# A decode block on one core: the last V loaded behind its predecessor, quads in fours, and gate and up computed as rows

## The chip, the cores and the metric

One core of one Trainium2 chip runs the whole program. The time is the device time of one execution in microseconds. A profiled execution also has a "span", from the first instruction to the last, which is about 2 us shorter than the time (659.4 for 661.2). All moments below, such as "650.3", are us from the start of the span.

## The reference, cut to what matters

It is one decode step for two sequences: layer norm, attention over a cache, output projection, layer norm, gated MLP.

```python
B, Sq, D = 2, 1, 512
Hq, Hkv, Sk, Dh = 32, 32, 8192, 128      # k_cache, v_cache: (2, 32, 8192, 128) bf16
F = 1376
q = layernorm(x) @ wq                    # wq (512, 4096)
p = softmax(q k^T * Dh ** -0.5)
h = x + (p v) @ wo                       # wo (4096, 512)
gate = layernorm(h) @ W_gate             # (512, 1376)
up = layernorm(h) @ W_up
out = h + (relu(gate) * up) @ W_down     # W_down (1376, 512)
```

There is one query per head, so the work is to read the cache once. The program reads 281.06 MB.

## The kernel before

The heads are handled in 16 "quads" (four heads of one sequence). Each quad has a K tile and a V tile of 8.4 MB each, 64 KB on every partition. VectorE (DVE) multiplies K by the query and folds the product down; ScalarE (ACT) takes the exponentials; TensorE (PE) multiplies them with V. There are two buffers for K and one for V.

```python
for n in range(N - 1):                        # N = 16
    scores(n, HALVES if n == 0 else (0, T))   # DVE: product, 4 folds, a reduction; ACT: exponentials
    if n + 2 < N:
        load_k(n + 2)
    collect()                                 # DVE + PE: eviction of a finished pair of quads
    # ... (row sums and gathers at certain n)
    weighted_v(n)                             # PE: 64 matmuls of 512 columns
    if n + 2 < N:
        load_v(n + 1)
# K buffer of quad 14, now free: wo, then the last V in four pieces, then gate, up, W_down
# ... (loads of wo: three blocks and one with 1 KB rows)
CUTS = (0, T // 2, T * 7 // 8, T * 15 // 16, T)
load_v(N - 1, CUTS)
# ... (loads of W_gate, W_up, W_down)
scores(N - 1)
# ... 28 of 32 "wo rows", then the pieces of the last V; its last eighth with V as the weights:
v_stationary(N - 1, o_b, CUTS[3], T)
normalize_last(L, o_b, zil)
for h in range(G):
    project(wol[:, h, :], ol[:, h, :], last=(h == G - 1))
```

A "wo row" is one matmul of the output projection: 512 columns of wo move past the attention output of the two tokens (tile `ar_ps`). The sum is then turned into columns (`a_ps` before, `h_ps` in the changed kernel), and layer norm and gate follow. `W` and `X` are the buffers of the weights that are loaded late. The last quad of each sequence is a special case: its own row sums, its own projection, and columns instead of rows. The MLP computes gate and up as columns: each 128x128 block of the weights is loaded as PE's stationary operand, and the two tokens are its moving columns. So the activations come out as W_down's product needs them.

```python
def mlp_in(g, ps):                            # 44 matmuls with two moving columns
    for c in range(KC):
        for fc in range(FC):
            # ...
            nc.tensor.matmul(out=ps[0:w, fc, :], lhsT=lhsT, rhs=hd[:, c, :], ...)
mlp_in(0, gate_ps); var = variance(hd_f, "ln2"); mlp_in(1, up_ps)
# ... relu, product
for fc in range(FC):                          # "y rows": 11 blocks of W_down, 4 matmuls each
    y_rows(act[0:w, fc, :], (wd_sb[:, fc, :] if fc < NF else wd_l[0:w]), last=(fc == FC - 1))
```

The softmax here doesn't subtract the row's maximum and nothing guards it: scores larger than these inputs give would overflow.

## Time and profile before

| before | value |
|---|---|
| time, median of 3 runs (661.32 to 661.61) | 661.44 us |
| span of the profiled run | 659.4 us |
| main DMA queue busy | 98.9% of the span |
| DVE busy | 92% |
| PE busy | 18% |

These are lines of the page: the span, the engines, the DMA queue, and the costliest group of DVE with its time, mean, and the idle time just before it.

```profile
span 659.4 us, 3234 instructions
...
PE 119.5 (18%) x1341; PEld 58.6 (9%) x1341; DVE 609.6 (92%) x225; ACT 55.8 (8%) x142; POOL 2.5 (0%) x8
...
q1 hardware_dynamic: 7272, 281.06, 98.9%
...
L222 DVE TENSOR_TENSOR k<-k,qrep 128x32768 bf16<-128x32768 bf16 (+1 forms) x17 | 275.7, 16217 | 8.9 <-DMA k<-in_A_k_cache_dram 8.8
```

Two resources look nearly full. The last line decides between them: DVE waited 8.8 us in all for K. The transfers are the bound.

The windows view of the same kernel shows the rate (the last number) in the loop and near the end; the number before it is the DMA share, and before that PE's granted clock, as a share of full speed.

```profile
core 0: us, PE busy (x) PEld busy (x) DVE busy (x) ACT busy (x) POOL busy (x), PEclk, DMA share, GB/s
40.00:554.00 514.00, 79.09 (x854) 35.70 (x854) 503.10 (x133) 38.46 (x104) 0.00 (x0) 0.57 1.00 433
645.00:650.00 5.00, 4.01 (x86) 3.10 (x79) 1.99 (x8) 0.00 (x0) 0.00 (x0) 0.78 0.97 399
650.00:655.00 5.00, 4.41 (x111) 4.10 (x114) 1.37 (x10) 0.00 (x0) 0.00 (x0) 0.50 0.71 269
```

433 GB/s is the steady rate of the loop, and close to the most there is: the Trainium skill, "DMA: Bandwidth & Descriptors", section "Specifications", gives 435 GB/s as the ceiling of the fabric, and the measured 433 agrees. 281.06 MB at 433 GB/s is 649 us. Only some 10 us of the span are left, for the start and for the end.

These are lines of the timeline before (start, duration, engine, line, operation, what ended the wait).

```profile
595.47 17.23 DVE L222 TENSOR_TENSOR k<-k,qrep 128x32768 bf16<-128x32768 bf16 x1 [1.24 <-DMA k<-in_A_k_cache_dram]
...
650.34 1.71 PE L510 MATMUL gate_ps<-hd,W 128*128 128x2 bf16 x44 [0.25 <-DVE hd L493]
652.34 1.72 PE L510 MATMUL up_ps<-hd,W 128*128 128x2 bf16 x44
654.09 0.24 DVE L528 TENSOR_TENSOR act<-gate,up_ps 96x2 bf16<-96x2 f32 x2 [0.94 <-PE up_ps L510]
654.38 1.55 PE L466 MATMUL y_ps<-W,act 128*2 128x128 bf16 x40 [0.33 <-DVE act L528]
655.76 0.28 PE L466 MATMUL y_ps<-wd_l,act 96*2 96x128 bf16 x4
656.09 0.29 DVE L535 CAST y_row<-y_ps 128x128 bf16<-128x128 f32 x1 [1.76 <-PE y_ps L466]
```

Two things end together. The chain of computation reaches the y rows at 654.38. The last full rows of W_down were issued at 641.99 and landed 13.5 us later, at 655.5; by the trace's landing records (the moments at which each of the 16 DMA engines reports its part of a load) the final 96 rows came at 655.7.

### The profile page before, as it was taken

The page shows a single profiled execution, that of the slowest core. Times are in us where ns is not written, and L with a number is a line of the kernel's source. Part 1 is how long each engine was busy: PE and PEld are TensorE (multiplying, and loading weights), DVE is VectorE, ACT ScalarE, POOL GpSimd, SP SyncE. Part 2 cuts the span into 40 slices and gives each one's busy share as a digit, 9 for nine tenths or more (in the row PEclk, how much of TensorE's full clock was granted, in tenths as well). Part 3 has the DMA queues.
Part 4 walks back from the last instruction along what each step waited for, and adds up shares of the span by engine and source line. Part 5 has one row for each costly group of instructions (what it writes and reads, how often), then busy time and mean ns, then how long its engine had stood idle before and what let it go on. Part 6 is the DMA issues. An engine that isn't in the chain of part 4 may idle for free.

```text
span 659.4 us, 3234 instructions
## 1 busy us (share of the span) xinstructions
PE 119.5 (18%) x1341; PEld 58.6 (9%) x1341; DVE 609.6 (92%) x225; ACT 55.8 (8%) x142; POOL 2.5 (0%) x8
## 2 busy tenths in 40 slices
PE   2100302003030210303012130301202030020446
PEld 1000101001010100101001110100001010010225
DVE  2899999999999999999999999999999998999952
ACT  2201001010101001010101001010010101001020
POOL 1000000000000000000000000000000000000000
PEclk9555755757565575756557575555757555575656
DMA  9999999999999999999999999999999999999996
GB/s 382 445 445 445 395 433 446 437 445 418 417 445 437 441 442 398 445 445 426 441 417 433 445 422 441 437 417 441 426 441 441 421 438 426 433 441 433 393 420 259
DMA packets 7314, 281.26 MB, mean 427 GB/s; under 512 B 802, under 2 KB 1412, under 8 KB 2308
## 3 DMA queue, kind: packets, MB, share of 16 engines
q1 hardware_dynamic: 7272, 281.06, 98.9%
q8 instruction: 10, 0.16, 0.1%
q14 instruction: 4, 0.03, 0.0%
q10 hardware_dynamic: 28, 0.01, 0.0%
HBM read 281.06 MB, written 0.00 MB: 426 GB/s over the span
## 4 chain that ended last, share of the span: by engine, by line
DVE 62%; DMA 33%; PE 3%; issue 1%; ACT 0%; DVEq 0%
DMA k<-in_A_k_cache_dram 31%; DVE k L222 29%; DVE k L228 28%; DVE sc L231 4%; DMA wq_sb<-in_A_wq_dram 2%; DVE osb L268 1%; DVE qrep L188 1%; PE qps L175 1%; PE o L257 1%; PE ar_ps L452 0%; ACT qrep L186 0%; PE y_ps L466 0%; PE a_ps L459 0%; PE gate_ps L510 0%; PE up_ps L510 0%
## 5 line engine op out<-in xcount | busy, mean ns | idle before, releaser
L222 DVE TENSOR_TENSOR k<-k,qrep 128x32768 bf16<-128x32768 bf16 (+1 forms) x17 | 275.7, 16217 | 8.9 <-DMA k<-in_A_k_cache_dram 8.8
L228 DVE TENSOR_TENSOR k<-k 128x16384 bf16<-128x16384 bf16 (+3 forms) x68 | 266.8, 3923 | 2.3
L257 PE MATMUL o<-v,pm 128*32 128x512 bf16 x1016 | 88.1, 522 | 395.8 <-DMA v<-in_A_v_cache_dram 395.8
L234 ACT ACTIVATE pm<-sc 32x256 bf16<-32x256 f32 x64 | 47.2, 738 | 563.9 <-DVE sc L231 527.6
L257 PEld LDWEIGHTS <-pm 128*32 128x32 bf16 x1016 | 37.9, 127 | 444.8 <-issue 282.3
L231 DVE TENSOR_REDUCE sc<-k 128x256 f32<-128x2048 bf16 (+1 forms) x17 | 36.7, 2161 | 1.6
L307 PE MATMUL rep<-osb,spread 128*64 128x128 f32 (+1 forms) x16 | 5.9, 474 | 110.5 <-DVE osb L268 110.5
L234 ACT ACTIVATION_READ_ACCUMULATOR pm<-sc 32x1 f32 x64 | 15.0, 234 | 0.0
L307 PEld LDWEIGHTS rep<-osb,spread 128*64 128x64 f32 (+1 forms) x16 | 3.2, 257 | 114.1 <-DVE osb L268 114.1
L188 DVE CAST qrep<-qps 32x512 bf16<-32x512 f32 x8 | 5.5, 692 | 7.2 <-ACT qrep L186 7.1
L266 DVE TENSOR_SCALAR osb<-o,turn_of 128x128 f32<-128x128 f32 x10 | 3.4, 344 | 9.2 <-PE o L257 9.2
L268 DVE SCALAR_TENSOR_TENSOR osb<-o,turn_of,osb 128x128 f32<-128x128 f32 x30 | 10.5, 351 | 1.1
L175 PE MATMUL qps<-wq_sb,xnb 128*64 128x512 bf16 x32 | 6.5, 562 | 7.0 <-DMA wq_sb<-in_A_wq_dram 4.8
L186 ACT ACTIVATE qrep<-qps 32x512 bf16<-32x512 f32 x8 | 4.7, 586 | 8.5 <-PE qps L175 5.2
L152 DVE COPY xc<-x_ps 128x8 f32<-128x8 f32 x1 | 0.2, 167 | 4.9 <-PE x_ps L149 4.9
L510 PEld LDWEIGHTS <-W 128*128 128x128 bf16 (+1 forms) x88 | 3.8, 126 | 0.3 <-issue 0.3
L175 PEld LDWEIGHTS <-xnb 128*64 128x64 bf16 x32 | 2.7, 147 | 10.0 <-issue 5.3
L452 PE MATMUL ar_ps<-W,oc 128*2 128x512 bf16 x28 | 3.2, 626 | 1.8 <-DVE oc L357 1.8
L297 PE MATMUL o_l<-lane_of,osb 128*128 128x4 f32 x2 | 0.6, 364 | 12.8 <-DVE osb L268 12.8
L317 DVE TENSOR_TENSOR rep<-rep,pick 128x128 f32<-128x128 f32 x6 | 1.8, 295 | 1.0 <-PE rep L307 0.9
L330 PE MATMUL zb<-zm,same 128*128 128x4 f32 (+2 forms) x12 | 2.3, 306 | 0.3 <-DVE ol_f L298 0.3
L330 PEld LDWEIGHTS zb<-zm,same 128*128 128x128 f32 x12 | 2.1, 258 | 0.8 <-issue 0.4
(92 smaller groups left out, 44.3 us busy)
## 6 DMA issues: line engine op xcount, KB each, us to landing
k<-in_A_k_cache_dram SPq DMA_DIRECT2D x2, 4096.0 KB
wq_sb<-in_A_wq_dram SPq DMA_DIRECT2D x1, 4096.0 KB, 12.3
v<-in_A_v_cache_dram SPq DMA_DIRECT2D x1, 4096.0 KB, 13.3
v<-in_A_v_cache_dram SPq DMA_DIRECT2D x1, 3072.0 KB, 20.2
W<-in_A_wo_dram SPq DMA_DIRECT2D x1, 2048.0 KB
W<-in_B_W_gate_dram SPq DMA_DIRECT2D x1, 1376.0 KB
W<-in_B_W_up_dram SPq DMA_DIRECT2D x1, 1032.0 KB, 27.4
W<-in_A_wo_dram SPq DMA_DIRECT2D x1, 1024.0 KB, 29.0
```

What stands on the lines that cost most here:

```text
L175: nc.tensor.matmul(out=qps[h * B * Q:(h + 1) * B * Q], lhsT=xnb[:, c].rearrange("p b q -> p (b q)"), rhs=wq_v[:, c, g:g + QP, h0 + h, :], ...
L186: nc.scalar.activation(out=dst, in_=src, func=ACT.Copy)
L188: nc.vector.tensor_copy(dst, src)
L222: nc.vector.tensor_tensor(out=kp, in0=kp, in1=_view(qrep[:, b, i, :], 0, [[0, hi - lo], [1, Dh]]), op=ALU.mult)
L228: nc.vector.tensor_tensor(out=kp[:, :, 0:half], in0=kp[:, :, 0:half], in1=kp[:, :, half:width], op=ALU.add)
L231: nc.vector.tensor_reduce(out=sc[:, lo:hi], in_=kp[:, :, 0:8], axis=AXIS.X, op=ALU.add)
L234: nc.scalar.activation(out=p_of[ps, :, :, h], in_=sc[ps, :].rearrange("p (g t) -> p g t", t=TG), func=ACT.Exp, accum_out=(zm[ps, b, i:i + ...
L257: nc.tensor.matmul(out=o[g:g + W2], lhsT=_view(pm, (0 if lane else R) + t // TG * W2, [[1, W2]]), rhs=vt[:, t:t + TG, :].rearrange("p t d ...
L268: nc.vector.scalar_tensor_tensor(out=osb, in0=o[:, t * Dh:(t + 1) * Dh], scalar=turn_of[:, t:t + 1], in1=osb, op0=ALU.mult, op1=ALU.add)
L307: nc.tensor.matmul(out=reps[where][at:at + m, max(k - 1, 0), :], lhsT=spread[n_of].rearrange("k u h m -> k (u h m)"), rhs=osb, start=True, ...
L330: nc.tensor.matmul(out=zb, lhsT=lhsT, rhs=z, start=True, stop=True)
L510: nc.tensor.matmul(out=ps[0:w, fc, :], lhsT=lhsT, rhs=hd[:, c, :], start=(c == 0 and fc == 0), stop=(c == KC - 1), skip_group_check=True)
```

## The change

Its intent is a simpler tail. The special last quad goes away: all quads are evicted in pairs and gathered in fours. To keep the last V off the end, each half of it is loaded as soon as PE has used the same half of its predecessor; wo then comes last before the MLP weights. The last K is scored in 3/4 and 1/4. Gate and up are computed as rows (the tokens stationary, 512 weight columns moving, three column groups side by side) and transposed by seven small matmuls.

```diff
-        weighted_v(n)
         if n + 2 < N:
-            load_v(n + 1)
+            weighted_v(n)
+            load_v(n + 1, (0, T) if n + 3 < N else HALVES)
@@ the last V, then wo (was: wo, then the last V)
+    vts[L] = vts[L - 1]
+    CUTS = (0, T // 2, T * 7 // 8, T)
+    for lo, hi in zip(HALVES[:-1], HALVES[1:]):
+        weighted_v(L - 1, lo, hi)
+        for a, b in zip(CUTS[:-1], CUTS[1:]):
+            if lo <= a < hi:
+                load_part(vts[L], A_v_cache, L, a, b)
+    for k in range(NGR):
+        load_wo(k)
@@ eviction of a pair
-        nc.vector.tensor_scalar_mul(osb, o[:, 0:Dh], turn_of[:, 0:1])
-        for t in range(1, TG):
-            nc.vector.scalar_tensor_tensor(...)
+        nc.vector.tensor_tensor(out=om..., in0=o..., in1=_view(turn_of, 0, [[1, TG], [0, Dh]]), op=ALU.mult)
+        nc.vector.tensor_reduce(out=osb, in_=om.rearrange("p (t d) -> p d t", d=Dh), ...)
@@ the MLP weights: a buffer of their own, the last K's, free only after its scores
+    X = kring.tile([P, RING], bf16, tag="k", name="X")
@@ MLP
+    def mlp_in(g, ps, c0=0, c1=KC):
+        for c in range(c0, c1):
+            for j in range(FT):
+                nc.tensor.matmul(out=ps[j * Q:(j + 1) * Q, :], lhsT=hd[:, c]...,
+                                 rhs=wgu[:, g, c, offs[j]:offs[j] + MT], ...)
+    ... seven matmuls act_ps <- act, ident; act_t = copy of act_ps on ACT
# cut: masks, row sums, the removed special cases of the last quad
```

## The prediction

> **What bounds the kernel now.** The DMA queue, for nearly the whole span. The page's queue table has the main queue busy for 98.9% of the span; the windows view gives 433 GB/s and DMA share 1.00 from 40 to 554 us, with a K or V load always outstanding. 281.06 MB at 433 GB/s is 649 us. DVE is 92% busy, but its first product of the last K (timeline, 595.47 us) waited for its DMA: one K takes DVE about 36 us, one K plus V takes DMA about 38.7. So only the end, or a hole in the queue, can change the time.
>
> **The tail before.** The last K lands at 595.4, V14 at 614.9, V15's last piece near 644.5, gate at 648.7, up at 652, the last W_down block near 655.5 (issue plus time to landing). From 636.4 PE is the chain: 28 wo rows 3.16, V15's first pieces, a_ps 2.0, the last V and projection until 649.1, mean, gate 1.71, variance, up 1.71 (ends 654.06), act, y rows 1.7, cast (ends 656.4), output to 659.4. Chain and DMA end within a microsecond of each other, so moving loads cannot gain more than about 1 us.
>
> **What the change does.**
> - Head: fewer mask and copy instructions on DVE, about 1.5 us. Worth 0: K2's issue still finds V0 in flight for 8 us.
> - Loop: the four evictions per pair (0.34+1.12 us) become a product and a reduce. DVE is not the bound: worth 0.
> - V15 follows V14 half by half; wo comes after it. V15's first half is issued near 609, before V14's second half lands at 615. V15 lands near 634.5, wo near 644.3; fewer short rows (the 1 KB wo rows go) may give 0.5 us. Gate, up and W_down now need the last K's buffer, free near 632, while the queue is full until 644: no hole.
> - The last K in 3/4 and 1/4: exponentials end near 634.5, V15's matmuls near 636.5, before wo's second half. Slack.
> - After wo: 16 rows 1.8, copy 0.7, h_ps 2.0, mean 0.8, hd 0.3: gate starts near 650.3, as before (650.34).
> - Gate and up as rows: each 12 matmuls of 512 columns, three side by side; at the measured 0.43 us per round of four, 4 x 0.43 = 1.7 each. As before.
> - Added: the product is 96x512 instead of 128x22, 0.6 for 0.24; seven transposes, 0.25+0.7+0.2; an ACT copy 0.3. About 1.8 us, all on the chain, because the y rows wait for it. W_down's last block has then landed.
>
> **Sum.** Before 659.4 span; +1.8 for row form and transposes; −0.5 for DMA; −0.5 because part of gate or up may run at the fast clock. The Trainium skill, "TensorE: Matmul & The Clock Gate", Part 1, puts warming at about 3.4 us of sustained work; this trace shows rounds of 0.43 us from 636.4 turning to 0.22 near 641. Predicted time 662.3 us, range 660.3 to 664.3; faster by over 2% 0.01, within 2% 0.98, slower 0.01.
>
> **What would show it.** Queue share about 0.99 and loop K issues 38.7 us apart as before; last V15 landing near 634.5; wo near 644; gate start near 650; first y row near 656 instead of 654.4; cast end near 658.
>
> **What would make it wrong.** A hole in the queue around 608 to 634 (V15 waiting for V14's halves) would add its length. If PE is fast from 645 on, gate and up halve and the kernel gains about 1 us instead.

## The result, and the profile after

The changed kernel takes 661.89 us (median of 6 runs, 661.39 to 662.11), the kernel before 661.38 in the same rounds. The ratio is 1.0006, with a 95% interval of 0.9993 to 1.0019. Here and below a ratio is the mean time of one kernel's runs over the mean of the other's in the same rounds, so it is not quite the ratio of the medians that are quoted.

The page after, the same lines as before, and one more (q8) that the last section needs:

```profile
span 660.1 us, 2931 instructions
...
PE 121.1 (18%) x1210; PEld 52.4 (8%) x1210; DVE 604.0 (92%) x163; ACT 59.6 (9%) x157; POOL 3.3 (1%) x14
...
q1 hardware_dynamic: 6600, 281.06, 98.8%
q8 instruction: 9, 0.15, 0.1%
...
L215 DVE TENSOR_TENSOR k<-k,qrep 128x32768 bf16<-128x32768 bf16 (+3 forms) x18 | 275.9, 15327 | 11.9 <-DMA k<-in_A_k_cache_dram 11.9
```

DVE does 5.6 us less and waits 3.1 us longer for K: what the loop gained went into a wait. The bytes are the same, and so is their rate, in the windows view after:

```profile
40.00:554.00 514.00, 78.23 (x844) 33.25 (x844) 500.96 (x102) 38.59 (x104) 0.00 (x0) 0.57 1.00 433
645.00:650.00 5.00, 4.04 (x30) 2.76 (x22) 0.44 (x3) 0.78 (x2) 0.00 (x0) 0.50 0.99 403
650.00:655.00 5.00, 4.21 (x31) 1.31 (x28) 2.55 (x8) 0.00 (x0) 0.00 (x0) 0.50 0.65 247
```

PE's clock, 0.78 from 645 to 650 before, is now 0.50. The end, in the timeline after:

```profile
644.17 1.88 PE L411 MATMUL ar_ps<-W,oc 128*2 128x512 bf16 x16 [3.14 <-DMA W<-in_A_wo_dram]
...
650.07 1.89 PE L456 MATMUL gate_ps<-X,hd 128*32 128x512 bf16 x12
...
652.30 1.89 PE L456 MATMUL up_ps<-X,hd 128*32 128x512 bf16 x12
...
654.24 0.68 DVE L474 TENSOR_TENSOR act<-gate,up_ps 96x512 bf16<-96x512 f32 x1 [0.70 <-PE up_ps L456]
...
655.69 1.34 PE L446 MATMUL y_ps<-X,act_t 128*2 128x128 bf16 x44 [0.28 <-ACT act_t L491]
657.08 0.29 DVE L497 CAST y_row<-y_ps 128x128 bf16<-128x128 f32 x1 [2.16 <-PE y_ps L446]
```

| moment | before | after | after minus before |
|---|---|---|---|
| last piece of the last V landed (landing records) | 644.5 | 634.2 | −10.3 |
| second half of wo landed (PE goes on) | long before | 644.1 | |
| first gate matmul | 650.34 | 650.07 | −0.27 |
| product of gate and up starts | 654.09 | 654.24 | +0.15 |
| first y row | 654.38 | 655.69 | +1.31 |
| last rows of W_down landed (landing records) | 655.7 | 655.7 | 0 |
| cast starts | 656.09 | 657.08 | +0.99 |
| end of span | 659.4 | 660.1 | +0.7 |

The last V is there 10 us earlier, and gate starts only 0.27 us earlier. wo took the last V's place as the thing that PE waits for. From gate to the first y row the row form takes 5.62 us instead of 4.04. Before, the rows ran into W_down's landing and finished 1.71 us after they began; after, they began when W_down had just come, and took 1.39.

### The profile page after: what moved, and what is told of

Read it like the earlier page. It is cut to its first block, busy times and chain, and to the rows that moved or that the text cites. A ratio compares the mean times of both kernels' runs of the same rounds, so it can differ in the third digit from the quotient of the medians.

```text
span 660.1 us, 2931 instructions
## 1 busy us (share of the span) xinstructions
PE 121.1 (18%) x1210; PEld 52.4 (8%) x1210; DVE 604.0 (92%) x163; ACT 59.6 (9%) x157; POOL 3.3 (1%) x14
## 3 DMA queue, kind: packets, MB, share of 16 engines
q1 hardware_dynamic: 6600, 281.06, 98.8%
## 4 chain that ended last, share of the span: by engine, by line
DMA 83%; PE 15%; ACT 0%; issue 0%; DVE 0%; SPq 0%
DMA v<-in_A_v_cache_dram 77%; PE o L249 13%; DMA W<-in_A_wo_dram 4%; DMA wq_sb<-in_A_wq_dram 2%; PE qps L166 1%; PE h_ps L423 0%; PE y_ps L446 0%; PE ar_ps L411 0%; PE up_ps L456 0%; ACT qrep L177 0%; PE gate_ps L456 0%; DVE qrep L179 0%; DVE act L474 0%; SPq L190 0%; ACT ar L419 0%
## 5 line engine op out<-in xcount | busy, mean ns | idle before, releaser
L215 DVE TENSOR_TENSOR k<-k,qrep 128x32768 bf16<-128x32768 bf16 (+3 forms) x18 | 275.9, 15327 | 11.9 <-DMA k<-in_A_k_cache_dram 11.9
L221 DVE TENSOR_TENSOR k<-k 128x4096 bf16<-128x4096 bf16 (+6 forms) x72 | 267.4, 3714 | 2.5
L249 PE MATMUL o<-v,pm 128*32 128x512 bf16 x1024 | 94.0, 544 | 415.9 <-DMA v<-in_A_v_cache_dram 408.2
L208 ACT ACTIVATE pm<-sc 32x256 bf16<-32x256 f32 (+2 forms) x68 | 48.1, 708 | 562.7 <-DVE sc L226 561.3
L226 DVE TENSOR_REDUCE sc<-k 128x256 f32<-128x2048 bf16 (+2 forms) x17 | 36.7, 2161 | 1.6
L292 PE MATMUL rep<-osb,spread 128*64 128x128 f32 x16 | 5.1, 421 | 101.5 <-DVE osb L262 101.5
L179 DVE CAST qrep<-qps 32x512 bf16<-32x512 f32 x4 | 2.8, 696 | 10.7 <-ACT qrep L177 10.7
L262 DVE TENSOR_REDUCE osb<-om 128x128 f32<-128x512 f32 x8 | 8.2, 1026 | 0.3
L258 DVE TENSOR_TENSOR om<-o,turn_of 128x512 f32<-128x512 f32 x8 | 5.5, 684 | 3.2 <-PE o L249 3.2
L177 ACT ACTIVATE qrep<-qps 32x512 bf16<-32x512 f32 x12 | 7.0, 588 | 5.1 <-PE qps L166 4.9
```

What stands on the lines that cost most here:

```text
L177: nc.scalar.activation(out=dst, in_=src, func=ACT.Copy)
L208: nc.scalar.activation(out=p_of[ps, lo // TG:hi // TG, :, h], in_=sc[ps, lo:hi].rearrange("p (g t) -> p g t", t=TG), func=ACT.Exp, accum_o ...
L215: nc.vector.tensor_tensor(out=kp, in0=kp, in1=_view(qrep[:, b, i, :], 0, [[0, hi - lo], [1, Dh]]), op=ALU.mult)
L221: nc.vector.tensor_tensor(out=kp[:, :, 0:half], in0=kp[:, :, 0:half], in1=kp[:, :, half:width], op=ALU.add)
L226: nc.vector.tensor_reduce(out=sc[:, lo:hi], in_=kts[n][:, lo:hi, 0:8], axis=AXIS.X, op=ALU.add)
L249: nc.tensor.matmul(out=o[g:g + W2], lhsT=_view(pm, (0 if lane else R) + t // TG * W2, [[1, W2]]), rhs=vt[:, t:t + TG, :].rearrange("p t d ...
```

## The experiments

The theory that was tested is called "two ends meet". The y rows need the chain of computation and the landing of W_down, and both come at about 655.5, so neither the row form nor a shorter chain can move the time by its full length. The main rival says that one of the two sets the end alone. Other runs test the order of the loads, the slack of DVE, and PE's clock. Each run was timed beside the kernel before on the same chip; that one took 661.33 in the first and third job and 661.28 in the second.

### Gate and up as columns in the changed kernel

```diff
-                nc.tensor.matmul(out=ps[j*Q:(j+1)*Q, :], lhsT=hd..., rhs=wgu[:, g, c, offs[j]:offs[j]+MT])
+                nc.tensor.matmul(out=ps[0:w, fc, :], lhsT=<128x128 block of wgu>, rhs=hd[:, c, :])
-    # seven transposes, copy on ACT
```

> The changed kernel with gate and up in the old column form (44 matmuls with two moving columns each, no transposes). Theory (two ends meet: the y rows need both the compute chain and the landing of W_down at 655.5 to 655.7 us): first y row near 654.2, but the last rows wait for the landing, cast ends near 656.2, time about 0.6 to 0.9 us below the changed kernel, near 661.1. Rival (the chain alone sets the end, W_down has long landed): the full 1.5 us come off, near 660.4.

Measured: 660.96 us (660.81 to 661.05), ratio to before 0.9994 (0.9982 to 1.0007). Its timeline:

```profile
654.13 1.74 PE L439 MATMUL y_ps<-X,act_t 128*2 128x128 bf16 x44 [0.33 <-DVE act_t L474]
655.92 0.29 DVE L481 CAST y_row<-y_ps 128x128 bf16<-128x128 f32 x1 [1.84 <-PE y_ps L439]
```

The first y row comes 1.56 us earlier than in the changed kernel, but the cast only 1.16. The rows take 1.74 instead of 1.34, because the last ones meet W_down, which landed at 655.5. The time is 0.93 below the changed kernel's median, though that one was timed in another job. The theory gave 0.6 to 0.9, the rival 1.5. This is the fastest correct version. All its five runs lie below all nine of the kernel before, but by 0.4 us, and the interval includes 1. It is no win that one could claim.

### Gate and up as rows in the kernel before

The reverse edit: row form and transposes, with before's loads and attention. (The query tile, gate, and three small tiles share buffers to fit.)

> The kernel before with only gate and up as rows and the seven transposes; loads and attention as before. Theory: gate starts near 650.5, first y row near 656 (1.6 us later than before), all of W_down has landed by then, time about 1 us above before, near 662.4. Rival (the transposes hide behind W_down's landing): same time as before, 661.4.

Measured: 661.64 us median, ratio 1.0013 (1.0001 to 1.0026). The five runs fall in two groups, 661.3 to 661.6 (three runs) and 663.1 to 663.4 (two), and the profile is of the second. None is within half a microsecond of the theory's 662.4, and the first group is near the rival's 661.4. These are the first half of the last V, gate and the y rows in the profiled run:

```profile
639.63 3.30 PE L260 MATMUL o<-v,pm 128*32 128x512 bf16 x32
...
651.34 1.89 PE L519 MATMUL gate_ps<-W,hd 128*32 128x512 bf16 x12 [0.38 <-DVE hd L501]
...
656.96 1.23 PE L469 MATMUL y_ps<-W,act_t 128*2 128x128 bf16 x40 [0.28 <-ACT act_t L553]
```

Gate started 1.0 us later than before. Some 0.3 of that was there when the wo rows began (636.69 instead of 636.38), and 0.6 more came from the first half of the last V, which took 3.30 instead of 2.71: the clock records show the fast clock from 642.46 here, and from 640.95 before. From gate to the first y row it took 5.62 us, exactly as in the changed kernel, and the last rows of W_down had landed at 656.5. So in this run the row form costs what it costs there, 1.58 us more than columns, and nothing hid behind W_down. The time rises by 0 to 2 us; why a run falls in one group or the other, and whether the fast group hides the transposes, one profile does not settle.

### No load of W_down, in the changed kernel and in the kernel before

```diff
-    for f, r in blocks: nc.sync.dma_start(out=wd_sb..., in_=B_W_down...)
-    nc.sync.dma_start(out=wd_l, in_=B_W_down[FULL:F, :])
-        y_rows(act_t[0:w, f, :], (wd_sb[:, f, :] if f < NF else wd_l), ...)
+        y_rows(act_t[0:w, f, :], wo_sb[0:w, f, :], ...)      # wrong result on purpose
```

> The changed kernel without any load of W_down (the y rows read wo's tile instead; wrong result on purpose). Theory: the chain from wo's landing arrives at the same moment as W_down, so 3.2 us less of transfers change the time by at most 0.5 us. Rival (the end of the transfers sets the time): about 3 us less.

> The kernel before without any load of W_down (wrong result on purpose). Theory: before, the last 12 y rows waited for the landing at 655.5 to 655.7; without it the rows run through from 654.4 and the cast ends about 0.4 us earlier: time 0.3 to 0.6 us below before. Rival (before was bound by its chain alone): no change. Second rival (bound by the transfers): about 3 us less.

Measured: the changed kernel without W_down 662.41 us (661.29 to 662.57), the kernel before without it 660.42 (659.61 to 661.01; ratio 0.9983, 0.9969 to 0.9996). The y rows and the cast of the changed kernel without W_down, then of the kernel before without it:

```profile
655.71 1.34 PE L441 MATMUL y_ps<-W,act_t 128*2 128x128 bf16 x44 [0.28 <-ACT act_t L486]
657.10 0.29 DVE L492 CAST y_row<-y_ps 128x128 bf16<-128x128 f32 x1 [2.16 <-PE y_ps L441]
```

```profile
654.34 1.34 PE L459 MATMUL y_ps<-W,act 128*2 128x128 bf16 x44 [0.33 <-DVE act L521]
655.74 0.29 DVE L528 CAST y_row<-y_ps 128x128 bf16<-128x128 f32 x1 [1.45 <-PE y_ps L459]
```

Taking 1.4 MB away, 3.2 us at the full rate, moves the changed kernel's cast by 0.02 us. There the chain has the last word. In the kernel before the cast comes 0.35 us earlier: its rows had indeed waited for W_down, and the wait was worth about a third of a microsecond. The times do not show this as cleanly. The kernel before without W_down is 0.9 us faster than with it (the theory gave 0.3 to 0.6), and the changed kernel without W_down has a median 0.5 us higher than with it, although its cast is at the same place. In the profiles these remainders lie after the cast: from its start to the end of the span the kernel before takes 3.3 us and 3.0 without W_down, the changed kernel 3.0 and 3.6. No run explains that stretch, so differences of half a microsecond are better read at the cast than in the time.

### wo before the last V again

```diff
+    for k in range(NGR): load_wo(k)
     L = N - 1
     # ... last V, half by half
-    for k in range(NGR): load_wo(k)
```

> The changed kernel with wo's two loads ahead of V15 (as before), nothing else changed. Theory: V15's last piece lands near 644.5 instead of 634.2 and the eviction, spread, gather and all 32 wo rows follow it: 16 matmuls 1.8, eviction 1.7, spread and normalising 1.4, 32 rows or their second half 1.9 to 3.7; after that the chain is the same. Time 4 to 6 us above the changed kernel, near 667. Rival (the order of these loads does not matter, as the total time of the transfers is the same): no change.

Measured: 666.02 us (665.88 to 666.67), ratio 1.0074. PE waits for the last V, not for wo:

```profile
641.78 3.53 PE L249 MATMUL o<-v,pm 128*32 128x512 bf16 x32 [3.71 <-DMA v<-in_A_v_cache_dram]
...
648.04 2.70 PE L410 MATMUL ar_ps<-W,oc 128*2 128x512 bf16 x32
...
654.75 1.90 PE L455 MATMUL gate_ps<-X,hd 128*32 128x512 bf16 x12
```

Gate starts 4.68 us later than in the changed kernel. So the order of these loads matters, by 4.1 us in the time (666.02 against 661.89), and the theory's 4 to 6 holds. This says what the first part of the change is for: with the last quad handled like every other, what follows its V (eviction, spread, gather, all wo rows) is 4 to 5 us longer than before's special case (from the last V's landing to gate 10.5 us here, 5.8 before), and loading that V ahead of wo buys these microseconds back. It buys nothing more.

### PE kept busy while it waits

```diff
+    idle = ps_mm.tile([P, TG * Dh], f32, tag="mm", name="idle")
+    keep_busy(3)   # 128x512 matmuls into idle, after the row sums
+    keep_busy(2)   # before the first 16 wo rows
+    keep_busy(7)   # while wo's second half is on its way
+    keep_busy(2)   # before h_ps
```

> The changed kernel with 14 unused matmuls (128x512) in PE's waits between 636 and 646 us, to keep its clock up. Theory: the fast clock holds into h_ps and gate, gate and up fall from 1.9 towards 1.0 us each if it holds to 652; then the first y row comes at 654 to 655, but the last rows still wait for W_down at 655.7: time 0.3 to 0.9 us below the changed kernel. If the clock drops again in h_ps (two moving columns per matmul), no gain: gate and up stay at 1.9 and the fillers cost up to 0.5 us. Rival (nothing waits for W_down): up to 2 us less.

Measured: 661.28 us (661.09 to 662.53), ratio 1.0004. The timeline:

```profile
649.12 1.60 PE L467 MATMUL gate_ps<-X,hd 128*32 128x512 bf16 x12
...
651.47 1.71 PE L467 MATMUL up_ps<-X,hd 128*32 128x512 bf16 x12 [0.34 <-DMA X<-in_B_W_up_dram]
...
655.72 0.42 PE L457 MATMUL y_ps<-X,act_t 128*2 128x128 bf16 x12 [0.25 <-DMA X<-in_B_W_down_dram]
```

The clock records of this run have the fast clock from 642.63 to 649.46, and the 16 wo rows of the second half fell from 1.88 to 1.03. The Trainium skill, "TensorE: Matmul & The Clock Gate", Part 1, says that the clock is granted after a busy window of about 3.4 us, in windows that run freely; here all intervals are multiples of 3.41 us, and the fast one began after a window (639.22 to 642.63) in which fillers and wo rows kept PE busy for all 3.41 us, so this trace agrees. The first y row came at 654.64, 1.05 earlier than in the changed kernel. But up now waited for W_up and the last 12 y rows for W_down, as the profile says itself. Of 1.05 us won by the chain, 0.89 reached the cast (656.19). The median is 0.61 us below the changed kernel's, within the theory's 0.3 to 0.9, but one run took 662.53, and the interval of the ratio to the kernel before (0.9991 to 1.0016) includes 1.

### Both: columns and fillers

> Column form and the fillers for PE's clock together. Theory (the landing of W_down at 655.5 is the floor once the chain is short enough): the first y row comes at 653 to 653.7, earlier than in the column kernel (654.13), but the cast still ends near 656.1: time 660.9, as the column kernel. Rival (the chain still counts): 0.5 to 1 us below it.

Measured: 661.21 us (660.94 to 661.51), as the columns alone within noise. But the run did not test the floor: wo's second half landed at 645.2 in its profile, 1.1 us later than in the changed kernel, so gate started at 650.79 and the first y row came at 654.73 and not at 653.5.

```profile
645.22 1.88 PE L419 MATMUL ar_ps<-W,oc 128*2 128x512 bf16 x16 [3.37 <-DMA W<-in_A_wo_dram]
...
654.73 1.34 PE L450 MATMUL y_ps<-X,act_t 128*2 128x128 bf16 x44 [0.33 <-DVE act_t L485]
```

The trace says where the gain went. By the landing records one DMA engine was late: fifteen of the 16 had landed wo by 643.76 (644.07 in the changed kernel), the last one at 645.18, after a packet of instructions at 642.98 (see the last section). And the clock was fast from 638.23 to 645.05, so that PE waited for wo through the second half of it. The y rows then ran through without a wait, so the chain set the end, and the floor stays untested.

### Larger rows for W_up and W_down; two queues

```diff
-    blocks = [(f, min(4, NF - f)) for f in range(0, NF, 4)]     # W_down rows of 4096, 4096, 2048 bytes
+    blocks = [(0, NF)]                                          # 10240 bytes per partition
-    for g, w, c0, c1 in (..., (1, B_W_up, 0, KC - 1), (1, B_W_up, KC - 1, KC)):
+    for g, w, c0, c1 in (..., (1, B_W_up, 0, KC)):
```

> The changed kernel in column form, with W_up in one load (11008 bytes per partition) and W_down's full rows in one load (10240 bytes per partition instead of 4096, 4096, 2048). Theory: if the 3 us between the first and the last engine's completion of the last loads come from their short rows, W_down lands 0.5 to 1 us earlier and the time is near 660.5, below both kernels. Rival (the skew has another cause): as e1_cols.

```diff
# column form; only W_down's loads change
-    nc.sync.dma_start(out=wd_..., in_=B_W_down...)
+    nc.scalar.dma_start(out=wd_..., in_=B_W_down...)
```

> Column form with W_down's four loads issued from ACT's queue, beside gate and up on SP's. Theory (the bytes and the slowest of the 16 engines decide when the last load lands): the last landing stays within 0.4 us of 655.5, time as the column kernel; up may land up to 1 us later, and then the chain waits for it. Rival (one queue of short loads is what drains slowly): last landing 0.5 to 1.5 us earlier, time near 660.3.

Both are misses as improvements. With larger rows: 662.78 us (ratio 1.0023). By the landing records the last load landed at 655.3, only 0.2 earlier than in the column kernel, with 3.4 us between the first and the last of the 16 engines, so short rows are not what spreads them. And the blocks of gate and up must now be read with a step of 10 elements, to match W_down's rows. The weight loads of the column kernel, then of this one (duration in ns: least, median, most):

```profile
L455 PEld LDWEIGHTS <-X x88: 102/117/291, 650.1 to 653.6; 128*128 128x128 bf16 x80, 128*96 128x96 bf16 x8
```

```profile
L455 PEld LDWEIGHTS <-X x88: 136/156/305, 650.0 to 655.5; 128*128 128x128 bf16 x80, 128*96 128x96 bf16 x8
```

The median goes from 117 to 156 ns, and gate from 1.74 to 2.76 us. The Trainium skill, "SBUF — State Buffer", in its note on cachelines, says that reads which leave a 16-byte line each time pay for it, so that steps up to 8 bf16 elements are free; a step of at most 4 in the column kernel against 10 here agrees with that, and no run tries a step between.

With two queues: 663.17 us (ratio 1.0028). The last landing was at 655.7, as the theory had it; its time, that of the column kernel, was missed by 2.2 us. W_down, issued from 633.15 on the second queue, no longer stood behind wo, and wo came later:

```profile
645.89 1.88 PE L411 MATMUL ar_ps<-W,oc 128*2 128x512 bf16 x16 [4.31 <-DMA W<-in_A_wo_dram]
...
654.78 1.74 PE L455 MATMUL up_ps<-hd,X 128*128 128x2 bf16 x44 [0.75 <-DMA X<-in_B_W_up_dram]
```

The rows of wo's second half start 1.8 us later than in the column kernel (644.09). The Trainium skill, "DMA: Bandwidth & Descriptors", section "Issuing engines are not separate DMA queues", says that loads from several issuing engines run on the same 16 DMA engines and interleave. This run agrees, and shows what that does to an order that one queue had kept.

### How much slack DVE has

```diff
# changed kernel; in each of the first 15 steps, the same sums once more for part of the columns
+        sums(n, sc, 0, T)          # first run: all;   later runs: T // 4,  T // 2
         sums(n, sc, 0, T)
```

> The changed kernel with the last reduction of each loop step done twice (2.29 us more of DVE in each of the first 15 steps, same result). Theory (DMA is the bound in the loop, DVE has about 2.4 us of slack per step): at most 2 us more, K loads still 38.7 us apart. Rival (DVE is the bound, 92% busy): 15 times 2.29, about 34 us more.

Measured: 680.30 us, ratio 1.0289. Both expectations fell: neither 2 nor 34 us, but 18.4 more than the changed kernel's 661.89. The slack of 2.4 us per step was a mistake of arithmetic. It compared a K's product, folds and reduction (about 36 us) with the transfers' 38.7, and forgot that every second step also has an eviction. In this run, where DVE never waits for a K, a step takes 39.5 us on average (K loads issued from 63.41 to 576.50 in 13 steps); take off 2.3 and the unpadded step is 37.2. Moreover DVE starts late: its first product begins at 23.9, after the query projection, and in the changed kernel it first waits for a K at 246.5, in its seventh step. Until then it is behind the transfers. The slack is therefore a sum over the whole run, the 11.9 us that the page shows DVE waiting for K. That made a new theory, with two runs to test it:

> The changed kernel with a quarter of the last reduction repeated in each of the first 15 steps (about 0.62 us each, 9.3 us of DVE in all, same result). New theory (DVE starts behind the transfers and catches up; its whole slack is the 11.9 us that it waited for K in the changed kernel's trace, not 2.4 us per step): the waits for K fall to about 2.6 us and the time stays within 0.5 us of the changed kernel. Rival (any DVE time is on the critical path): 9 us more.

> The changed kernel with half of the last reduction repeated in each of the first 15 steps (about 1.22 us each, 18.3 us in all). New theory: 11.9 us vanish in the waits for K, the last K's scores end about 6.4 us later, about 5 us of that vanish while PE waits for wo's second half; the time is 1 to 3 us above the changed kernel, near 663.5. Rival (slack of 2.4 us per step): no change. Rival (all on the path): 18 us more.

Measured: 662.41 us with a quarter (661.88 to 662.84) and 664.31 with half (664.02 to 664.52). The K tile's own view in the first of them:

```profile
its engine sat idle before it (us, times) until:
  DMA k<-in_A_k_cache_dram: 2.7, 2
```

In the second no such wait is left.

| added to DVE | waits for K | last K's scores end | time | above the changed kernel |
|---|---|---|---|---|
| 0 | 11.9 | 632.6 | 661.89 | |
| about 9.3 us | 2.7 | 633.0 | 662.41 | 0.5 |
| about 18.3 us | 0 | 638.6 | 664.31 | 2.4 |
| about 34 us | 0 | 654.6 | 680.30 | 18.4 |

The first 9 us vanish in the waits: 11.9 less 9.3 is 2.6, measured 2.7. Beyond 11.9, the scores end later (6.0 us for 18.3 added), and some 3.6 us of that (the expectation said about 5) vanish once more, in the time that PE spends waiting for wo's second half. Then every microsecond counts.

## Why the prediction was right

The forecast was 662.3 (660.3 to 664.3) and "within 2%"; measured were 661.89 and a ratio of 1.0006.

- **The transfers bound the kernel: right.** Queue share 98.8% after 98.9%, 433 GB/s in both, and K issues 38.7 us apart from 283 us on, when DVE had caught up.
- **No hole in the queue: right.** The last V's first half was issued at 608.39, before the second half of its predecessor landed (PE went on at 614.73). In stretches of 5 us from 600 to 645 the DMA share is 0.96 to 1.04. The last V landed at 634.2 (predicted 634.5), wo at 644.1 (644.3).
- **Gate starts as before: right,** at 650.07 against a predicted 650.3. The run with wo first shows that the reordering is worth 4 us, all of which is needed to pay for the simpler last quad.
- **Row form and transposes cost 1.8: nearly right.** From the first gate matmul to the first y row it took 1.58 more: 0.42 before the product starts, 0.44 in the product (0.68 instead of 0.24), 0.72 in transposes and copy. The prediction had 0, 0.36 and 1.45 for these three, so its 1.8 is near because two errors cancel in part: gate and up were no longer equal to the columns, and the transposes were cheaper. The first y row was predicted near 656 and came at 655.69. Columns put back won 1.56 there.
- **Faster clock, −0.5: wrong.** PE's clock stayed at 0.50 from 638.7 to the end, and gate and up took 1.89 each, not 1.7 or less. The waits for wo (0.78 and 3.14 us) left PE idle, and filling them brought the fast clock. They are not the whole account: in one window of the clock, 648.97 to 652.38, PE was busy for 3.35 of 3.41 us, and the clock stayed slow all the same. The fillers showed that the clock can be had, and that 0.89 us of it reach the cast.
- **Transfers, −0.5: half wrong.** wo landed 0.37 us earlier than the last V had, but W_down landed when it did before.
- **The cast near 658: too late.** It came at 657.08, to end at 657.37. Before, the y rows had lost about a third of a microsecond to W_down's landing (the run of before without W_down), and the changed kernel did not lose it. The prediction had charged 1.7 us for them; they took 1.34. This partly makes up for the clock's missing 0.5.
- **The sum: near, and in part by luck.** At the cast the runs give 1.58 for the row form, less 0.27 for the earlier gate and 0.32 for the y rows that no longer wait: 0.99. The prediction had 1.8 less two times 0.5, which is 0.8. One of its credits failed and the other half failed, and a gain that it did not have came in. Of the 0.99 us at the cast, 0.7 are left at the end of the span and 0.5 in the medians, and no run says why the stretch after the cast was shorter.
- **DVE is not the bound, so its savings are worth 0: right, but for too generous a reason.** "One K takes DVE about 36 us" left out the evictions. The slack is 11.9 us in the whole run, not 2.4 us in each step; a change that had added 18 us instead of removing 5.6 would have been mispredicted.

## What to carry to other kernels

When a kernel is bound by one stream of transfers, list what each late arrival still has behind it, and load last what has the shortest remainder; while the last landing stays where it is, a shorter chain can win back at most the distance from its end to that landing. For the kernel before that was under half a microsecond: its cast came at 656.09, and the earliest one seen with all loads in place, in the column kernel, at 655.92. Count the slack of the second busiest engine as the sum of its waits over the run, not as a difference per step, because an engine that starts late uses up its first steps catching up. And when two chains meet at one moment, test each by taking away the other, as shortening either one alone shows only part of its length.

## What the Trainium skill lacked or had wrong

- "DMA: Bandwidth & Descriptors": no figure for how far the 16 engines drift apart on one queue. By the landing records, the first and the last engine finished the last load of W_down 3.0 us apart in the changed kernel, and 3.4 us with rows of 10240 bytes. The traces point to a cause. The packets of the q8 line on the profile's page are marked as instructions; each is 16 KB and takes about 1.1 us. In the changed kernel all 16 engines land a load within 0.4 us until the first such packet, at 77.6; in the next load one engine is 1.2 us behind the other fifteen. After the second, at 155.1, two engines are late, and after the eighth, at 609.0, eight land 1.5 us or more after the first. After the ninth, at 648.0, one engine alone is 1.4 us behind the rest to the end: fifteen had landed the last rows of W_down by 654.35, it came at 655.70. No run removed these packets, so this is read from the traces and not tested.
- "TensorE: Matmul & The Clock Gate", section on LDWEIGHTS: its formula knows only the number of columns. Reading the same 128 columns with a step of 10 elements instead of at most 4 took 156 ns instead of 117. The cacheline note that agrees with this is on the page "SBUF — State Buffer".
- "TensorE: Matmul & The Clock Gate", Part 1: right about the window of 3.4 us, but it gives no measure of how busy a window must be. The busy time of the profile does not give one either. In the changed kernel the window from 631.90 to 635.31, with 2.82 us busy, was followed by the fast clock, and the window from 648.97 to 652.38, with 3.35 us busy, was not. The first held only matmuls with 512 moving columns, the second also narrower ones; whether that is the reason is not shown.
